# A three-layer mixer on one core: another order for the last batch of the first phase, and another buffer for w_ch

## The chip, the cores and the metric

The kernel runs on one core of a Trainium2 chip. The metric is the device time of one execution in microseconds. Three timed runs of the kernel before gave 1033.99, 1036.04 and 1035.72 us; the median is 1035.72 us.

## What is computed

The reference has eight batches of 576 tokens and 512 channels and three layers, each fed by the one ahead of it:

```python
q_s = softmax(q, axis=-1); k_s = softmax(k, axis=2)
x = q_s @ (k_s^T @ v)                       # by head; heads side by side: 576 x 512
u, v = split(relu(x @ w_in))                # 512 + 512 channels
v_n = (v - mean(v)) / sqrt(var(v) + 1e-6)
x = (u * (w_spatial @ v_n + b_spatial)) @ w_out
theta = x @ w_theta
y = w_tok_r @ (x * cos(theta)) + w_tok_i @ (x * sin(theta))
u = x + y
out = u + relu(u @ w_ch)
```

## The kernel before, in words

All products keep near fp32 accuracy: an operand is held as a high part in fp32r and a low part (`three`, L196), and a product is three matmuls. Weights are split on the chip once; those of the last layer wait in DRAM (`th_d`, `ch_d`, `op_d`).

The program has two phases. The first goes over the batches b = 0 to 7 (`run`, L1103) and does attention and the gated layer; its result, called y, goes to DRAM in four stores per batch (`y_out`, L656). The second goes over the batches again (`step2`, L1090) and does the last layer. The order of all work is written by hand, as words in strings: `PLANS`, `PLAN` and `LAST` (L33 to L75) for the first phase, `PLAN2` and `LAST2` (L57 to L68) for the second. Each word calls one function, and each engine works through its instructions strictly in the order in which the words issue them. A word that waits on an engine therefore holds up all later words on that engine; a DMA that POOL or SP issues stands in the queue of that engine too.

`LAST` is the plan of batch 7 of the first phase. There is no next attention to prepare, so it also carries the first steps of the second phase's batch 0, as words with an H ahead. Its words, in the order of the data:

- V, v, N: the five token tiles of x times the right half of w_in, relu, statistics and normalisation. U, r: the left half of w_in. S, G: the spatial product and the gate. Y, y: the product with w_out (`y_mm`, L647) and its store (`y_out`, L656: an ACT copy out of PSUM at L659, a DMA on SP at L660).
- ldy0, ldy1, ldr: loads of y of batches 0 and 1. th: the load of w_theta into the half of w_in's buffer that V has used (L1031). tok: the loads of the first token operators w11 and t2, of the rows that are left over and of their differences (L1032 to L1036, all DMAs of POOL).
- Hm0 to Hm4: theta of the five token tiles (`th_mm`, PE, L194). Hw, Ht, Hr: the turns, the reduction and the sine and cosine (L743 to L768, ACT and DVE). Hy: four transposes of y on PE (`th_y`, L774). Hz: the products x cos and x sin (`th_z`, DVE, L781, L782; tile 4 at L789). Hs, Hn, Hp, Hi, Hk, HI, HL: sums and the splits into high and low parts (L794 to L841, on ACT, DVE and POOL). Tile 4 holds the left-over tokens of two batches.

The scratch tiles of `t2` (L169) are nine buffers used in a ring: who takes one waits for the last user, a DMA that stores from it among them. In the first phase PSUM has three double banks (`big`, L163), used by S, Y and Hy among others, and two single banks for theta. Behind `LAST` the PSUM pools are made anew (L1130), and two operators that stay for the whole second phase are loaded over the gate's buffer (L1129).

The second phase does seven token products per batch (Q0 to Q6, `product`, L843, PE L867), then the product with w_ch in four parts (C0 to C3, `ch_mm`, L909; its weights are listed by `ch_pairs`, L902). The split parts zr and zi of x cos and x sin of tiles 2 and 3 lie in w_in's buffer for batch 0 and in w_out's for the later ones (`zs`, L666). w_ch is loaded once, in batch 0, by the word ldc (L1069) into the part of w_in's buffer in which those parts of batch 0 lie.

Of the kernel before, what the change touches and what calls it, by code (L numbers as in the profile page):

```python
# [17 lines left out]
P = 128  # L18
# [37 lines left out]
}  # L56
PLAN2 = (  # L57
# [5 lines left out]
)  # L63
# [4 lines left out]
)  # L68
LAST = (
# [5 lines left out]
)  # L75


OPS = ("w11", "t2", "w21", "t3", "t1", "t4", "w22")
# [3 lines left out]
def kernel(  # L82
# [15 lines left out]
    nc = tc.nc  # L98
    B = q.shape[0]
    S = w_tok.shape[2]  # L100
    D = 64
    DM = w_out.shape[2]
# [32 lines left out]
    w4_all = fix.tile([P, 8, 1024], F32R, name="w4")  # L135
    sp_all = fix.tile([P, 10, S], F32R, name="sp")
    g_all = fix.tile([P, 8, S], F32R, name="g")
    w4 = [w4_all[:, i, :] for i in range(8)]
    sp_w = [sp_all[:, i, :] for i in range(10)]
    g_s = [g_all[:, i, :] for i in range(8)]  # L140
    wo_all = fix.tile([P, 4, 1024], F32R, name="wo")
    wo = [wo_all[:, i, :] for i in range(4)]
# [13 lines left out]
    ch_d = dram.tile([P, 8, 512], F32R, name="ch_d")  # L156
# [21 lines left out]
    def f(ap):  # L178
        return ap.bitcast(F32)
# [16 lines left out]
    def three(a, w):  # L196
        return [(a[0], w[0]), (a[0], w[1]), (a[1], w[0])]
# [465 lines left out]
    y1 = [t.rearrange("p (k s) -> p k s", k=NK) for t in (qb, kb)]  # L663
    z_rem = [vn[8:10]]

    def zs(b, t):  # L666


        if t < 2:
            z = vn[4 * t:4 * t + 4]  # L670
        else:
            z = [w[:, 0:DM] for w in w4[4 * t - 8:4 * t - 4]]
            if b:
                z = [w[:, h * DM:(h + 1) * DM] for w in wo[2 * t - 4:2 * t - 2] for h in range(2)]
        return z[0:2], z[2:4]


# [10 lines left out]
    def op_load():  # L688
        n = turn["load"]
        if n < B * len(TURNS):  # L690
            nc.gpsimd.dma_start(out=op_buf[n % 2], in_=op_d[TURNS[n % len(TURNS)]])
            turn["load"] += 1
# [15 lines left out]
    th = {"phase": 0}  # L708
# [83 lines left out]
    LO, UP = slice(0, DM // 2), slice(DM // 2, DM)  # L792
# [20 lines left out]
    def th_hi(b, t):  # L813
        if t < NT:
            nc.scalar.copy(out=s2[t][0], in_=th["s2", b, t])
            nc.scalar.copy(out=zs(b, t)[0][0], in_=th[b, t][1])
        else:
            for full, z in zip(th[b, t], z_rem):
                nc.scalar.copy(out=z[0], in_=full)

    def th_zi_hi(b, t, eng):
        z, r = zs(b, t)[1][0], th[b, t][0]
        if eng is nc.gpsimd:
            eng.tensor_scalar(out=z, in0=r, scalar1=1.0, scalar2=0.0, op0=ALU.mult, op1=ALU.add)  # L824
        else:
            nc.scalar.copy(out=z, in_=r)

    def th_lo(b, t, eng):
        if t < NT:
            z, w = zs(b, t)[0], th[b, t][1]  # L830
            eng.tensor_tensor(out=z[1], in0=w, in1=f(z[0]), op=ALU.subtract)  # L831
        else:
            for full, z in zip(th[b, t], z_rem):
                nc.vector.tensor_tensor(out=z[1], in0=full, in1=f(z[0]), op=ALU.subtract)
# [58 lines left out]
    def s_late(b, n, t, hi, eng=None):  # L893
# [5 lines left out]
        else:  # L899
            eng.tensor_tensor(out=z[1], in0=x, in1=f(z[0]), op=ALU.subtract)  # L900

    def ch_pairs(m):  # L902
        pairs = []
        for kk in range(NK):
            w = w4[kk][:, m * P:(m + 1) * P], w4[4 + kk][:, m * P:(m + 1) * P]
            pairs += three(w, (st["uh"][:, kk, :], qt_s[kk]))
        return pairs

    def ch_mm(b, m):  # L909
        th["c", m] = big()  # L910
        acc(th["c", m], ch_pairs(m))
# [14 lines left out]
    def ch_half(b, m, h):  # L926

        c = (A, B_)[h]
        ps = bank()[:, A]
        acc1(ps, [(a, x[:, c]) for a, x in ch_pairs(m)])  # L930
        o = t2()[:, A]
        nc.vector.scalar_tensor_tensor(
            out=o, in0=ps, scalar=0.0, in1=y1[b % 2][:, m, c], op0=ALU.max, op1=ALU.add
        )
        nc.sync.dma_start(out=out[b, m][:, c], in_=o)
# [4 lines left out]
    w1 = {}  # L940
    for i in range(8):
        c = slice(i * P, (i + 1) * P)
# [5 lines left out]
    for i in range(NK):  # L948
        c, d = slice(i * P, (i + 1) * P), slice(DM + i * P, DM + (i + 1) * P)
# [39 lines left out]
    def hv(fl):  # L989
# [76 lines left out]
        "ldr": lambda b, i, fl: load_rem(b + 2),  # L1066
        "ldy": lambda b, i, fl: load_y(b + 2),
        "b": lambda b, i, fl: op_load(),
        "ldc": lambda b, i, fl: b or [  # L1069
            nc.gpsimd.dma_start(out=w4_all[:, :, c], in_=ch_d[:, :, c]) for c in (LO, UP)  # L1070
        ],
        "C": lambda b, i, fl: ch_mm(b, i),
        "o": lambda b, i, fl: ch_out(b, i, eng(fl, nc.vector)),
        "x": lambda b, i, fl: ch_half(b, i % 4, i // 4),
# [138 lines left out]
```

## Time and profile before

| what | us |
|---|---|
| median of three timed runs | 1035.72 |
| the profiled execution, its own time | 1033.3 |
| span of that profile | 1031.5 |
| busy: PE, DVE, ACT, POOL | 963.0, 783.7, 480.4, 505.0 |

The span is the time from the first instruction to the last. PE is busy for 93% of it. The page cuts the span into 40 slices of 25.8 us and gives each engine's busy tenths: PE's row has 9 nearly everywhere, 7 in the slices 22 and 23 (567 to 619 us) and 8 in slice 25. Batch 7 of the first phase runs from 520.8 to 606 us, batch 0 of the second from there to 665.2 us. A group's idle time before it and what ended it stand in brackets in the timeline.

### The profile page before, as it was taken

The numbers are of one execution on the slowest core, as the hardware profiler recorded it, in microseconds if no ns is written. First come the engines' busy times: TensorE is split into PE (matmuls) and PEld (weight loads), VectorE is DVE, ScalarE is ACT, GpSimd is POOL, SyncE is SP. The second block draws the span as 40 slices with busy tenths as digits, with TensorE's granted clock in tenths as the row PEclk, the third lists the DMA queues.
The fourth block names the chain that finished last, engine by engine and source line by source line (L and its number), as shares of the span: only waits on it lengthen the run. The fifth ranks groups of instructions, "written<-read, shape, count | busy, mean of one in ns | idle before, by whom it ended". The sixth has DMA issues, their size and how long they took to land.

```text
span 1031.5 us, 16589 instructions
## 1 busy us (share of the span) xinstructions
PE 963.0 (93%) x6496; PEld 908.4 (88%) x6496; DVE 783.7 (76%) x1156; ACT 480.4 (47%) x821; POOL 505.0 (49%) x502
## 2 busy tenths in 40 slices
PE   4587999999999999999999779899999999999998
PEld 3566899999899998999999669898999989998997
DVE  7888867778878788776435667879888878887874
ACT  3645546543555445554324443345454545354520
POOL 6366147555546565435112443637374645645460
PEclk9989999999999999999999989999999999999999
DMA  7541441425545175330150355642726253534432
GB/s 265 202 133 46 165 159 39 162 73 184 173 147 202 68 238 170 129 133 19 45 198 12 138 200 175 179 170 92 240 90 232 82 203 118 200 122 162 138 139 92
DMA packets 49998, 147.84 MB, mean 143 GB/s; under 512 B 8320, under 2 KB 23936, under 8 KB 40832
## 3 DMA queue, kind: packets, MB, share of 16 engines
q1 hardware_dynamic: 40464, 92.16, 25.7%
q0 software_dynamic: 9456, 54.63, 15.6%
q8 instruction: 51, 0.84, 0.3%
q14 instruction: 27, 0.22, 0.1%
HBM read 113.38 MB, written 33.39 MB: 142 GB/s over the span
## 4 chain that ended last, share of the span: by engine, by line
PE 58%; DVE 5%; POOL 4%; DMA 4%; issue 3%; ACT 1%; DVEq 0%; POOLq 0%; ACTq 0%
PE ps L186 25%; PE ps L867 15%; PE pb L194 9%; PE ps L194 5%; DMA sp<-op_t 2%; PE ps L446 1%; PE pb L774 1%; DMA y<-t 1%; DMA w<-ch_d 1%; PE ps L528 1%; DVE wo L831 1%; POOL s L811 1%; DMA sp<-op_w 1%; POOL s L810 0%; POOL wo L824 0%
## 5 line engine op out<-in xcount | busy, mean ns | idle before, releaser
L186 PE MATMUL ps<-sp,vn 128*128 128x288 f32 x896 | 127.9, 300 | 6.0 <-ACT vn L609 2.7
L186 PEld LDWEIGHTS ps<-sp,vn 128*128 128x128 f32 x896 | 121.7, 191 | 7.3 <-ACT vn L609 2.9
L186 PE MATMUL ps<-g,wo 128*128 128x288 f32 x768 | 109.2, 300 | 5.2 <-ACT t L659 4.6
L186 PEld LDWEIGHTS ps<-g,wo 128*128 128x128 f32 x768 | 104.6, 191 | 7.1 <-ACT t L659 5.7
L186 PE MATMUL ps<-xh,w 128*128 128x288 f32 x512 | 94.4, 302 | 9.1 <-ACT w L279 7.7
L194 PE MATMUL ps<-w,xh 128*128 128x512 f32 x320 | 97.5, 397 | 3.6 <-ACT t L581 2.8
L186 PEld LDWEIGHTS ps<-xh,w 128*128 128x128 f32 x512 | 78.0, 192 | 11.0 <-ACT w L279 7.9
L186 PE MATMUL ps<-uh,w 128*128 128x288 f32 x448 | 81.8, 299 | 3.7 <-DMA w<-ch_d 3.7
L194 PE MATMUL pb<-w,xh 128*128 128x512 f32 x256 | 80.3, 395 | 0.0
L194 PEld LDWEIGHTS ps<-w,xh 128*128 128x128 f32 x320 | 59.1, 188 | 17.5 <-ACT t L581 3.5
L186 PEld LDWEIGHTS ps<-uh,w 128*128 128x128 f32 x448 | 67.7, 191 | 4.9 <-DVE t L757 4.1
L645 POOL TENSOR_TENSOR g<-t,g 128x576 fp32r<-128x576 f32 x19 | 28.6, 1504 | 73.6 <-ACT g L644 73.5
L810 POOL TENSOR_TENSOR s<-t,t 128x256 f32<-128x256 f32 x32 | 25.1, 784 | 79.0 <-DVE t L805 79.0
L867 PE MATMUL ps<-sp,vn 128*128 128x288 f32 x360 | 59.3, 298 | 2.8 <-DMA sp<-op_w 1.2
L747 ACT ACTIVATE t<-pb 128x512 f32<-128x512 f32 x36 | 21.6, 599 | 73.6 <-PE pb L194 57.2
L186 PE MATMUL ps<-xl,w 128*128 128x288 f32 x256 | 55.7, 300 | 0.0
L194 PEld LDWEIGHTS pb<-w,xh 128*128 128x128 f32 x256 | 46.8, 188 | 9.6
L867 PEld LDWEIGHTS ps<-sp,vn 128*128 128x128 f32 x360 | 50.9, 188 | 4.2 <-issue 2.3
L644 ACT CAST g<-t 128x576 fp32r<-128x576 f32 x32 | 21.5, 673 | 69.6 <-DVE t L643 69.5
L867 PE MATMUL ps<-sp,s 128*128 128x288 f32 x384 | 53.7, 295 | 0.0
L867 PEld LDWEIGHTS ps<-sp,s 128*128 128x128 f32 x384 | 52.4, 188 | 0.6
L523 POOL TENSOR_TENSOR qb<-qb,q_s 128x512 f32<-128x512 f32 (+1 forms) x40 | 38.7, 1000 | 25.3 <-DVE q_s L517 21.6
(263 smaller groups left out, 2552.1 us busy)
## 6 DMA issues: line engine op xcount, KB each, us to landing
sp<-op_t POOLq DMA_DIRECT2D x24, 1152.0 KB, 5.7
sp<-op_w POOLq DMA_DIRECT2D x16, 1152.0 KB, 5.5
vb<-in_v SPq DMA_DIRECT2D x8, 1300.0 KB, 7.5
y<-t SPq DMA_DIRECT2D x32, 288.0 KB, 2.3
qb<-in_q SPq DMA_DIRECT2D x7, 1152.0 KB, 5.2
out<-t SPq DMA_DIRECT2D x28, 288.0 KB, 2.1
kb<-in_k SPq DMA_DIRECT2D x6, 1152.0 KB, 5.1
st<-in_w_tok SPq DMA_DIRECT2D x9, 576.0 KB, 4.0
```

The costliest lines, as they stand in the source:

```text
L186: nc.tensor.matmul(out=ps[:, c, 0:CH], lhsT=a, rhs=w[:, c * CH:(c + 1) * CH], start=first and i == 0, stop=final and i == last,)
L194: nc.tensor.matmul(out=ps, lhsT=a, rhs=w, start=(i == 0), stop=(i == last))
L446: nc.tensor.matmul(out=o, lhsT=kb[p, c0:c0 + P], rhs=v4[p, r, 2 * j:2 * j + 2, :].rearrange("p h e -> p (h e)"), start=(r == 0), stop=(r = ...
L523: eng.tensor_tensor(out=x, in0=x, in1=m.to_broadcast(list(x.shape)), op=ALU.mult)
L528: nc.tensor.transpose(ps[:, r * P:(r + 1) * P], qb[:, r * 512 + j * P:r * 512 + (j + 1) * P], ident)
L644: nc.scalar.copy(out=g_s[m], in_=g)
L645: eng.tensor_tensor(out=g_s[4 + m], in0=g, in1=f(g_s[m]), op=ALU.subtract)
L747: nc.scalar.activation(out=w, in_=ps, func=ACTF.Copy, scale=INV_2PI, bias=MAGIC)
L774: nc.tensor.transpose(yn[:, j * P:(j + 1) * P], y, ident)
L810: eng.tensor_tensor(out=th["s4"][:, t, :], in0=r[:, LO], in1=x, op=ALU.subtract)
L811: eng.tensor_tensor(out=th["s1"][:, t, :], in0=x, in1=w[:, LO], op=ALU.add)
L867: nc.tensor.matmul(out=ps[:, m, 0:CH], lhsT=a, rhs=x, start=i == 0, stop=i == len(pairs) - 1)
```

## The change

The plan `LAST` is another table. In it y's load of batch 0 stands first; the token products V, U and the theta steps of the tiles are interleaved in another way; the spatial products S2 and S3 stand ahead of the theta products Hm2 to Hm4, tok stands behind them on PE; and some steps go to other engines (a letter v sends a step to DVE, p to POOL, c to ACT). Second, w_ch is loaded into w_out's buffer by one DMA, and ldc stands earlier in batch 0 of `PLAN2`, behind the second operator load. Third, zr and zi of the tiles 2 and 3 lie in w_in's buffer for every batch.

```diff
 PLAN2 = (
...
-    "J3 b1 f3 e0 g2 G2v g1 g3 G1v i4c' d0 y0 J1 f2 y1 h0 Q3 g0 G0v J0 m0 w0 G3 F3v e1 a2v Q4 t0 r0 "
+    "J3 b1 ldc f3 e0 g2 G2v g1 g3 G1v i4c' d0 y0 J1 f2 y1 h0 Q3 g0 G0v J0 m0 w0 G3 F3v e1 a2v Q4 t0 "
...
 LAST = (
-    "V0 v0 V1 V2 v1 N0v B0p v2 V3 V4 v3 ldr th U0 r0 U1 v4 r1 N1 N2 U2 N3 N4v rsp B U3 r2 r3 ldy0 "
...
+        "ldy0 V2 v2 V0 v0 U1 N2v r1 V1 v1 N1v N0c V4 V3 v3 th U0 ldr v4 N4 B0 P0v B0s E0 E1v P E0 E1v "
...
     def zs(b, t):
...
             z = [w[:, 0:DM] for w in w4[4 * t - 8:4 * t - 4]]
-            if b:
-                z = [w[:, h * DM:(h + 1) * DM] for w in wo[2 * t - 4:2 * t - 2] for h in range(2)]
...
+    ch_w = wo_all.rearrange("p k (h c) -> p (k h) c", h=2)
+
     def ch_pairs(m):
...
-            w = w4[kk][:, m * P:(m + 1) * P], w4[4 + kk][:, m * P:(m + 1) * P]
+            w = ch_w[:, kk, m * P:(m + 1) * P], ch_w[:, 4 + kk, m * P:(m + 1) * P]
...
-        "ldc": lambda b, i, fl: b or [
-            nc.gpsimd.dma_start(out=w4_all[:, :, c], in_=ch_d[:, :, c]) for c in (LO, UP)
-        ],
+        "ldc": lambda b, i, fl: b or nc.gpsimd.dma_start(out=ch_w, in_=ch_d),
```

Between the plans the line numbers of the changed kernel shift by one or two. How the instructions stand on three engines follows; g is the gate's result, wo w_out's buffer, w_76 w_in's, sp the buffer of the spatial weights and then of the token operators, qb y of batch 0, yr the left-over tokens, vn, w_76 and s the split parts, t a scratch tile with its number.

PE at the end of `LAST`, before, from the last theta product to the first token product (L867):

```order
L194 MATMUL pb<-w_76,kvl 128x512
L186 MATMUL ps<-g,wo 128x288 x24
L774 MATMUL ps<-turned,qb 128x128 x4
L186 MATMUL ps<-g,wo 128x288 x24
L774 MATMUL ps<-turned,qb 128x128 x4
L186 MATMUL ps<-g,wo 128x288 x24
L774 MATMUL ps<-turned,yr 128x128 x4
L186 MATMUL ps<-g,wo 128x288 x24
L867 MATMUL ps<-sp,vn_80 128x288 x2
```

And now:

```order
L195 MATMUL pb<-w_76,kvl 128x512
L772 MATMUL ps<-turned,qb 128x128 x4
L187 MATMUL ps<-g,wo 128x288 x24
L772 MATMUL ps<-turned,qb 128x128 x4
L187 MATMUL ps<-g,wo 128x288 x72
L772 MATMUL ps<-turned,yr 128x128 x4
L865 MATMUL ps<-sp,vn_80 128x288 x2
```

The transposes of tile 4 (yr) stood ahead of the last of w_out's four products and stand behind it now; the other transposes stand ahead of the second product, with nothing between the last three.

POOL around the loads of tok, before, from the last gate on:

```order
L645 TENSOR_TENSOR g<-t_5652,g 128x576
L810 TENSOR_TENSOR s_5712<-t_5556,t_5713 128x256
L811 TENSOR_TENSOR s_5711<-t_5713,t_5557 128x256
L824 TENSOR_SCALAR vn_82<-t_5556 128x512
L838 TENSOR_TENSOR vn_83<-t_5556,vn_82 128x512
L691 DMA sp<-op_w_101 128x2304
L691 DMA sp<-op_t_102 128x2304
L1034 DMA sp<-rem_d 128x1152
L1035 DMA yr<-diff_d 128x576
L810 TENSOR_TENSOR s_5712<-t_5642,t_5773 128x256
```

And now:

```order
L646 TENSOR_TENSOR g<-t_5528,g 128x576
L689 DMA sp<-op_w_101 128x2304
L689 DMA sp<-op_t_102 128x2304
L1034 DMA sp<-rem_d 128x1152
L1035 DMA yr<-diff_d 128x576
L829 TENSOR_TENSOR vn_81<-t_5575,vn_80 128x512
L829 TENSOR_TENSOR vn_85<-t_5568,vn_84 128x512
L839 TENSOR_TENSOR s_5700<-t_5738,s_5700 128x256
L808 TENSOR_TENSOR s_5702<-t_5667,t_5849 128x256
```

The four loads stood behind the first tile's sums and splits on POOL and stand ahead of all of them now; the only thing that the first of them waits for is the last spatial product, whose weights it overwrites.

ACT behind the first copy of y out of PSUM, before, with tile 4's first step at L747:

```order
L816 CAST vn_80<-t_5557 128x512
L659 COPY t_5759<-ps 128x576
L747 ACTIVATE t_5768<-pb 128x512
L766 ACTIVATE t_5705<-t_5704 128x512
L767 ACTIVATE t_5704<-t_5704 128x512
L768 ACTIVATE t_5705<-t_5705,half_pi 128x512
L815 CAST s_5710<-t_5773 128x256
```

And now, with tile 4's first steps at L745 and L752:

```order
L660 COPY t_5766<-ps 128x576
L824 CAST vn_82<-t_5574 128x512
L813 CAST s_5700<-t_5738 128x256
L814 CAST vn_84<-t_5568 128x512
L824 CAST vn_86<-t_5567 128x512
L764 ACTIVATE t_5736<-t_5735 128x512
L765 ACTIVATE t_5735<-t_5735 128x512
L766 ACTIVATE t_5736<-t_5736,half_pi 128x512
L745 ACTIVATE t_5843<-pb 128x512
L660 COPY t_5845<-ps 128x576
L752 ACTIVATE t_5843<-t_5843 128x512
```

Seven steps now come between the first copy of y (t_5766) and tile 4's first step (t_5843), which takes that copy's scratch buffer; the second copy of y (t_5845) stands behind it.

## Rows read from the trace of the kernel before

**Rows 1.** The page's first line.

```profile
span 1031.5 us, 16589 instructions
```

**Rows 2.** Chain of waits: start us, us, engine, output and line, instructions; DMA: what landed.

```profile
520.78 13.07 PE ps L194 x56
533.86 20.25 PE ps L186 x152
554.11 5.61 PE pb L194 x24
559.72 7.45 PE ps L186 x56
...
576.45 3.21 PE ps L186 x24
580.40 9.92 DMA y<-t
...
639.60 8.66 DMA w<-ch_d
```

**Rows 3.** Timeline, end of the first phase: start, us, instruction [idle before <- what ended it].

```profile
577.35 1.29 POOL L838 TENSOR_TENSOR vn<-t,vn 128x512 fp32r<-128x512 f32 x1
577.62 1.57 DVE L758 SCALAR_TENSOR_TENSOR t<-t,t 128x512 f32<-128x512 f32 x1
578.59 0.65 POOL L691 DMA_DIRECT2D sp<-op_w  x1
...
590.45 0.69 DVE L757 SCALAR_TENSOR_TENSOR t<-t,pb 128x512 f32<-128x512 f32 x1 [7.18 <-DMA y<-t]
591.17 0.69 DVE L758 SCALAR_TENSOR_TENSOR t<-t,t 128x512 f32<-128x512 f32 x1
...
595.42 1.09 PE L774 MATMUL ps<-turned,yr 128*128 128x128 f32 x4 [8.54 <-issue]
...
600.33 4.84 PE L186 MATMUL ps<-g,wo 128*128 128x288 f32 x24 [3.82 <-ACT t L659]
...
605.95 0.40 PE L867 MATMUL ps<-sp,vn 128*128 128x288 f32 x1 [0.78 <-ACT t L659]
```

**Rows 4.** Timeline, PE at the first product with w_ch.

```profile
648.39 0.82 PE L186 MATMUL ps<-uh,w 128*128 128x288 f32 x2 [3.67 <-DMA w<-ch_d]
...
649.49 1.16 PE L186 MATMUL ps<-uh,w 128*128 128x288 f32 x4
...
653.46 0.69 PE L186 MATMUL ps<-uh,w 128*128 128x288 f32 x4
```

**Rows 5.** Busy time by stretch: PE, PEld, DVE, ACT, POOL, granted clock, DMA share, GB/s.

```profile
590.00:600.00 10.00, 1.09 (x4) 0.72 (x4) 9.33 (x15) 3.88 (x8) 4.90 (x6) 0.50 0.00 1
...
520.80:606.00 85.20, 72.06 (x441) 65.83 (x440) 49.28 (x83) 35.29 (x61) 29.35 (x33) 0.92 0.32 108
606.00:665.20 59.20, 54.75 (x364) 51.73 (x364) 41.41 (x56) 23.57 (x45) 27.70 (x31) 0.97 0.63 200
721.00:773.10 52.10, 51.93 (x353) 49.12 (x353) 44.54 (x65) 24.73 (x47) 26.27 (x28) 1.00 0.48 165
```

**Rows 6.** DMA issues from 500 to 700 us: count, size, median us to landing.

```profile
y<-t SPq DMA_DIRECT2D x8, 288.0 KB, 2.2
...
w<-th_d POOLq DMA_DIRECT2D x1, 2048.0 KB, 9.2
```

**Rows 7.** Groups by line from 575 to 608 us: count | busy, mean ns.

```profile
L789 DVE TENSOR_TENSOR t<-t,ps 64x512 f32<-64x512 f32 x4 | 2.7, 684 | 0.1
L659 ACT COPY t<-ps 128x576 f32<-128x576 f32 x4 | 2.5, 638 | 5.9 <-PE ps L186 5.9
...
L767 ACT ACTIVATE t<-t 128x512 f32<-128x512 f32 x3 | 1.9, 632 | 0.1
...
L815 ACT CAST s<-t 128x256 fp32r<-128x256 f32 x4 | 1.6, 394 | 3.7 <-DVE t L805 3.7
...
L805 DVE TENSOR_TENSOR t<-t,t 128x256 f32<-128x256 f32 x3 | 1.3, 425 | 0.2
```

More of the change, by code (lines that the diff above doesn't have):

```diff
@@ L69 @@
 LAST = (
[5 rows of a table removed]
-)
[6 rows of a table added]
+    )
 OPS = ("w11", "t2", "w21", "t3", "t1", "t4", "w22")
```

11 rows, old and new, of tables (LAST, PLAN2) are left out of this document.

## The prediction

> **What bounds the kernel now.** I read the page first: a span of 1031.5 us [rows 1] in an execution of 1033.3 us, so 1.8 us lie around the span and I leave them as they are. The chain of waits shows what ends last: from 520.78 us, where batch 7 of the first phase begins on PE, it is PE work without a gap for 55 us [rows 2]. Then it stops being PE: a store of y takes 9.92 us in the chain, and later the load of w_ch takes 8.66 us [rows 2]. The busy time by stretch shows how much is at stake: 72.06 busy us in the 85.20 us of the last first-phase batch, 54.75 in the 59.20 us of the first second-phase batch, but 51.93 in 52.10 us for a later batch of the same work [rows 5]. So only these two stretches have something to give.
>
> The timeline names the holes. POOL issues the token loads at 578.59; the store of y's first part, 288 KB, starts behind them at 580.40 and lands 9.92 us later, where the median of such stores is 2.2 us [rows 2, 3, 6]. DVE's L757 for tile 4 has to take that store's scratch buffer and waits 7.18 us, until 590.45 [rows 3]. All that DVE has behind it (tile 3's products, which free a PSUM bank) waits too, and PE stands for 8.54 us before tile 4's transposes, 3.82 us before the last w_out product and 0.78 us before the first token product [rows 3]. Behind the waits the clock is low: granted 0.50 in 590 to 600 us, the level of 1.2 GHz [rows 5]; the 24 matmuls that take 3.21 us at 2.4 GHz [rows 2] take 4.84 [rows 3], 1.6 us more. In the next batch PE waits 3.67 us for w_ch, and then four matmuls take 1.16 us where four later ones take 0.69 [rows 4]; I take another 1.6 us for that.
>
> **PE's own work in the last batch.** The work is the same before and after. From the chain [rows 2]: V 13.07, U with S0 and S1 20.25, two theta products 5.61, S2 and S3 7.45; three more theta products at half of 5.61 each, 8.41; four w_out products at 3.21, 12.84; five sets of transposes at about a third of 1.09 us each (that row ran at half clock and its end overlaps), 1.75. Sum 69.4 us. The batch took 605.95 - 520.78 = 85.2 us, so 15.8 us were lost: 13.1 us of the three waits, about 2 us of slow clock, the rest small.
>
> **The new order, stage by stage.** Times stand on the clock of the trace of before.
>
> V, U and S. V2 goes first instead of V0, which needs no more than V0 did. The splits of vn are what S0 waits for, and they are spread over ACT, DVE and POOL now. The last of them, vn7 on POOL, comes about 0.2 us before S0 asks for it when I add up ACT's queue; a 512-wide step of POOL is 1.29 us [rows 3], so this costs 0 to 1.3 us, and I take 0. The load of w_theta is issued behind V3, about 541 us, and lands 9.2 us later [rows 6], 550; the first theta product comes at 554.1. Y's load stands first on SP, some 20 us ahead of its first reader: nothing.
>
> Theta, S2, S3. PE order is two theta products, S2 and S3, three theta products. The gate's DVE and ACT steps for S0 and S1 fall into 551 to 556 us and so free PSUM before S2 and S3 ask. Nothing is added. The token loads are now issued when S3 ends, about 567.5, instead of 578.59. In the trace everything of them and the store were through 11.7 us after the first issue (590.3 - 578.59), so now they are through at about 579.3.
>
> w_out's products. Through the first one PE is at 520.78 + 13.07 + 20.25 + 5.61 + 7.45 + 8.41 + 3 x 0.35 + 3.21 = 579.8. The second needs the first one's bank, which the ACT copy (0.64 [rows 7]) gives back: PE waits to 580.6, with one set of transposes inside the wait. Three products of 3.21 follow, to 590.2. Their banks come from tile 2's products (DVE, about 583.5, asked for at 583.8) and the second copy (586, asked for at 587).
>
> The store of the first part leaves at 580.6, behind loads that are through, and lands 2.2 us later, 582.8. Tile 4's first ACT step takes its buffer, but seven steps stand ahead of it: six of 0.63 and one of 0.39 [rows 7], to 584.7. So the wait that cost 7.18 us has 1.9 us to spare.
>
> The new tail. From 584.7 ACT does tile 4's first step, the second copy and L752, 1.9 us, to 586.6. DVE then does L755 to L757 (0.69 + 0.69 + 0.43 [rows 3, 7]) to 588.4, one short split 0.42, tile 3's two products 1.36, to 590.2: this frees the bank for tile 4's transposes, just when PE has finished w_out. Then come L802, L803 (0.85), L829 (0.68) and the four products of tile 4 at 0.68 [rows 7], to 594.5. The first token product waits for these, since the new PSUM pools need the old banks, so PE stands from 590.6 on. **This is the stall that takes the place of the old ones.** The second pair of these products takes the buffer of the third copy; that store leaves at 591.1 and lands at 593.3, which adds 0.2 us.
>
> What the rows say of DVE beside POOL: L758 took 1.57 us while POOL's L838 ran for 1.29, against 0.69 alone [rows 3]. In 582 to 591 us POOL now has steps of this kind. Bounds: 0, and all of POOL's work there, three 512-wide steps of 1.29 and three half as long, 5.8 us. Ahead of L755 DVE is through at about 585.2 and waits for ACT until 586.6, which takes up 1.4 us of such holds, so I take 1.5 us, nearer to the low end. The token product starts at 594.7 + 1.5 = 596.2, against 605.95: 9.75 us gained. PE has then stood for over 5 us and I charge one slow start, 1.6 us (bounds 0 and 2).
>
> **The first batch of the second phase.** w_ch's load is issued behind the second operator load, some 35 us before its first reader; 8.66 us [rows 2] are far inside. The wait of 3.67 us and its slow start of 1.6 go: 5.3 us. The check from the other side: the batch from its twelfth matmul (605.95 + 1.6) to 665.2 is 57.6 us, a later batch 52.1 [rows 5], a difference of 5.5. One DMA for two saves POOL under 1 us, off the path. On the 16 DMA engines the load now runs beside the operator loads that Q3 and Q4 need: 0 to 8.66 us. The operator of Q4 is issued before it and needed about 11 us later, so I take 0.
>
> From batch 1 on, zr and zi lie in the other buffer with the same readers and the same order of waits: nothing.
>
> **Sum:** 9.75 - 1.6 + 5.3 = 13.45 us, so 1033.3 - 13.45 = 1019.9 us. The timed runs lie 0.7 to 2.7 us above the profiled execution; by their median it would be 1022.3. I say 1021, and put the other cases on the same level, 1.1 above their sums.
>
> **Rivals.**
>
> *The port between DVE and POOL (1025).* If every POOL step of the tail holds DVE for its full length, 5.8 us instead of 1.5, the token product starts 4.3 us later: 1024.2, on the level 1025. For it: L758 ended just behind L838 [rows 3]. Against: the gap of 1.4 us there. The Trainium skill, page "SBUF — State Buffer", section "Who interferes with whom", says that a DVE step with two SBUF inputs and a GpSimd step that reads SBUF exclude each other for a whole instruction; by that rule this case would hold wherever the two meet. The trace agrees at the one place shown.
>
> *A store still behind loads (1028).* If the first or the third store takes 9.92 us again, tile 4 ends 7.7 us later: 1027.6, on the level 1028. It needs loads that last to 581 us, or the gate's buffer to be reloaded before 593; POOL comes to that reload only behind tile 3's sums, about 593.5, so the margin is the length of one store.
>
> *w_ch moves its wait (1026).* If its load holds up Q3 or Q4 for as long as C0 waited, the 5.3 us come back: 1025.2, on the level 1026.
>
> *The order is worth nothing (1035).* A wait in V, U or S that I took for covered eats the gain: w_theta or the splits of vn late by over 10 us. Every row speaks against it, since the margins are small but the waits are short.
>
> *Slower: the clock (1044).* After the stall of 5 us the clock is at 1.2 GHz. In the trace of before it is back within the next 24 matmuls (1.6 us lost of 3.2 possible [rows 3]). If it stayed low in the first token batch, each us of its 52 us of PE work [rows 5] would cost one more. From 13.5 us of such work on nothing is gained, half a batch gives 1019.9 - 1.6 + 26 = 1044. Before, granted clock is 0.97 in that batch [rows 5], so there is no sign of it. The Trainium skill, page "TensorE: Matmul & The Clock Gate", section "HAM oscillation — how this bites in real kernels", describes a kernel in which short bursts between waits kept falling back to the low clock. No such row stands here.
>
> **Numbers.** Forecast 0.55; port 0.18; store 0.13; w_ch 0.06; nothing gained 0.04; slower 0.04. A difference of 0.2% (2 us) is about what a measurement can tell. Faster: 0.55 + 0.18 + 0.13 + 0.06 = 0.92; same 0.04; slower 0.04. The range goes from 1016 (no hold of DVE by POOL and no slow start, 3.1 us less than the sum, near 1017.8, less a little of unknown spread) to 1029 (the store).
>
> **What would show it.** Right: no DVE wait on a store of y of more than 1 us; w_out's last three products without a gap over 0.5 us; one PE wait of 4 to 7 us before the first token product, ended by DVE's products of tile 4; no PE wait on w_ch; that batch near 53.5 us. Wrong: a PE wait in V to S3, a store of y over 5 us, a wait on an operator load in Q3 or Q4, or a granted clock under 0.9 in the whole first token batch.

## The result, and the profile after

The changed kernel takes 1019.31 us in the median of four runs (1018.24 to 1020.64), the kernel before 1035.88 us beside it. The ratio is 0.9843 with an interval of 0.9824 to 0.9861: 14 to 18 us faster. The forecast was 1021, with a range of 1016 to 1029. The four runs of the kernel before lie rather high here: beside the later runs its median was 1033.7 to 1034.53 us, and by a repeat of the changed kernel (e5 below) the gain is 12 to 17 us.

The profiled execution took 1020.64 us. The page of the changed kernel, its first line and PE's total, which was 963.0 us before: PE does the same work and stands less.

```profile
span 1018.9 us, 16589 instructions
...
PE 962.1 (94%) x6496; PEld 907.6 (89%) x6496; DVE 779.2 (76%) x1158; ACT 484.8 (48%) x828; POOL 495.5 (49%) x496
```

The chain of waits of the changed kernel (start us, us, engine, output and line, instructions), the counterpart of [rows 2]:

```profile
523.42 5.60 PE ps L195 x24
...
556.73 2.81 PE pb L195 x12
...
594.68 0.68 DVE t L787
596.09 0.69 DVE t L787
596.79 0.70 DVE t L787
597.73 11.95 PE ps L865 x78
...
650.60 0.76 DVE t L920
651.35 0.90 DVE w L829
```

No DMA stands in this stretch of it any more. Batch 7 of the first phase starts at 523.42 and the first token product at 597.73: 74.31 us, against 605.95 - 520.78 = 85.17 before. The chain leaves PE behind the second theta product and runs through DVE and ACT up to tile 4's products (L787).

The waits of PE from 520 to 665 us in the changed kernel (engine, line, what it waited for: us, times, longest):

```profile
PE ps L865 <- DVE t L787: 4.0, 1, 4.0
PE ps L187 <- ACT t L660: 0.3, 1, 0.3
```

Before, there were five: 8.5, 3.8, 0.8, 3.7 [rows 3, 4] and 0.7 us for a token operator. Now one of 4.0 us is left. The timeline of the changed kernel around it, several engines together (start, us, instruction [idle before <- what ended it]):

```profile
570.00 0.62 POOL L689 DMA_DIRECT2D sp<-op_w  x1 [13.95 <-PE ps L187]
...
583.42 11.07 SPq L661 DMA_DIRECT2D y<-t  x4
583.45 9.84 PE L187 MATMUL ps<-g,wo 128*128 128x288 f32 x72 [0.29 <-ACT t L660]
...
588.71 0.69 DVE L755 SCALAR_TENSOR_TENSOR t<-t,pb 128x512 f32<-128x512 f32 x1
...
593.13 0.60 PE L772 MATMUL ps<-turned,yr 128*128 128x128 f32 x4
594.68 2.80 DVE L787 TENSOR_TENSOR t<-t,ps 64x512 f32<-64x512 f32 x4
597.73 1.78 PE L865 MATMUL ps<-sp,vn 128*128 128x288 f32 x6 [4.01 <-DVE t L787]
599.31 1.53 PE L865 MATMUL ps<-sp,w 128*128 128x288 f32 x6
...
602.29 3.36 PE L865 MATMUL ps<-sp,s 128*128 128x288 f32 x24
```

The token loads are issued at 570.00, y's first store at 583.42. DVE takes up tile 4 at 588.71 with no wait in brackets, where [rows 3] had 7.18 us. The last three products with w_out run through (72 matmuls in 9.84 us). PE then stands from 593.7 until L787 is done, and the first token matmuls are slow: 4.56 us from 597.73 to 602.29 for 24 of them, with a granted clock of 0.52 from 597.7 to 600.7 us, the level of 1.2 GHz in nearly all of that stretch. The DMA issues of the changed kernel from 568 to 585 us (count, KB each, us to landing):

```profile
sp<-op_w POOLq DMA_DIRECT2D x1, 1152.0 KB, 5.5
sp<-op_t POOLq DMA_DIRECT2D x1, 1152.0 KB, 7.7
sp<-rem_d POOLq DMA_DIRECT2D x1, 576.0 KB, 8.6
yr<-diff_d POOLq DMA_DIRECT2D x1, 288.0 KB, 8.8
y<-t SPq DMA_DIRECT2D x1, 288.0 KB, 2.1
```

The last load is issued at 571.66 and lands at 580.5; the store leaves 3 us later and takes 2.1 us, not 9.92. The busy time by stretch of the changed kernel (PE, PEld, DVE, ACT, POOL, granted clock, DMA share, GB/s), the counterpart of [rows 5]:

```profile
523.40:597.70 74.30, 70.03 (x441) 64.09 (x439) 43.83 (x80) 39.18 (x68) 22.57 (x29) 1.00 0.39 131
597.70:651.40 53.70, 53.67 (x359) 51.34 (x360) 42.60 (x61) 23.91 (x46) 24.36 (x27) 0.97 0.57 207
```

**A yardstick.** Single runs of one kernel spread by 1 to 7 us, so in each profile I also read two stretches that do not contain the start of the program: A, from the first matmul of batch 7 to the first token product, and B, from there to the DVE split (L829 here, L831 before) for which the next batch's first product waits. Before: A = 85.17, B = 664.36 - 605.95 = 58.41, together 143.58 us. After: 74.31 + 53.62 = 127.93. So 15.65 us come from these two stretches: 10.86 from the first, 4.79 from the second. The two profiled times differ by only 1033.3 - 1020.64 = 12.7 us, because this execution came to batch 7 2.64 us later, through code that the change doesn't touch (see the last section), and took 0.35 us more behind B.

### The profile page after: what moved, and what is told of

The parts are those of the page before. It is cut to its first block, busy times and chain, and to the rows that moved or that the text cites. A ratio compares the mean times of both kernels' runs of the same rounds, so it can differ in the third digit from the quotient of the medians.

```text
span 1018.9 us, 16589 instructions
## 1 busy us (share of the span) xinstructions
PE 962.1 (94%) x6496; PEld 907.6 (89%) x6496; DVE 779.2 (76%) x1158; ACT 484.8 (48%) x828; POOL 495.5 (49%) x496
## 4 chain that ended last, share of the span: by engine, by line
PE 55%; DVE 9%; POOL 5%; DMA 2%; issue 2%; ACT 1%; DVEq 0%; POOLq 0%; ACTq 0%
PE ps L187 21%; PE ps L865 17%; PE pb L195 8%; PE ps L195 5%; PE ps L447 1%; DVE t L802 1%; PE pb L772 1%; DMA sp<-op_t 1%; POOL s L808 1%; POOL w L822 1%; PE ps L529 1%; DMA qb<-in_q 1%; DVE t L779 1%; POOL s L809 1%; DVE t L756 1%
## 5 line engine op out<-in xcount | busy, mean ns | idle before, releaser
L187 PE MATMUL ps<-uh,wo 128*128 128x288 f32 x448 | 80.8, 296 | 0.0
L187 PEld LDWEIGHTS ps<-uh,wo 128*128 128x128 f32 x448 | 66.8, 188 | 0.9
L745 ACT ACTIVATE t<-pb 128x512 f32<-128x512 f32 x36 | 21.5, 598 | 70.7 <-PE pb L195 54.4
L808 POOL TENSOR_TENSOR s<-t,t 128x256 f32<-128x256 f32 x30 | 23.8, 792 | 64.2 <-DVE t L803 64.2
L646 POOL TENSOR_TENSOR g<-t,g 128x576 fp32r<-128x576 f32 x17 | 25.4, 1495 | 56.5 <-ACT g L645 56.4
L865 PE MATMUL ps<-sp,w 128*128 128x288 f32 x288 | 48.8, 301 | 3.9 <-DVE w L829 3.4
```

What stands on the lines that cost most here:

```text
L187: nc.tensor.matmul(out=ps[:, c, 0:CH], lhsT=a, rhs=w[:, c * CH:(c + 1) * CH], start=first and i == 0, stop=final and i == last,)
L646: eng.tensor_tensor(out=g_s[4 + m], in0=g, in1=f(g_s[m]), op=ALU.subtract)
L745: nc.scalar.activation(out=w, in_=ps, func=ACTF.Copy, scale=INV_2PI, bias=MAGIC)
L808: eng.tensor_tensor(out=th["s4"][:, t, :], in0=r[:, LO], in1=x, op=ALU.subtract)
L865: nc.tensor.matmul(out=ps[:, m, 0:CH], lhsT=a, rhs=x, start=i == 0, stop=i == len(pairs) - 1)
```

## The experiments

| run | kernel | A | B | A + B | median us |
|---|---|---|---|---|---|
| | before | 85.17 | 58.41 | 143.58 | 1035.88 |
| | changed | 74.31 | 53.62 | 127.93 | 1019.31 |
| e1 | new `LAST` alone | 74.32 | 62.47 | 136.79 | 1024.07 |
| e2 | w_ch's move alone | 84.47 | 53.02 | 137.49 | 1027.7 |
| e3 | changed, token loads late | 81.02 | 53.91 | 134.93 | 1025.58 |
| e4 | before, own buffer for y | 79.05 | 60.28 | 139.33 | 1029.53 |
| e5 | changed, again | 74.33 | 53.94 | 128.27 | 1019.25 |
| e6 | changed, own buffer for y | 74.07 | 53.84 | 127.91 | 1018.47 |
| e7 | changed, PE kept busy | 74.34 | 52.34 | 126.68 | 1018.29 |
| e8 | bank for tile 4, early loads | 70.77 | 54.39 | 125.16 | 1015.75 |
| e9 | e8 with a quiet POOL | 70.77 | 53.82 | 124.59 | 1014.85 |
| e10 | e8, again | 70.77 | 54.41 | 125.18 | 1014.47 |

The kernel before ran beside each set of runs: 1033.8 us beside e1 to e4, 1033.7 beside e5 to e8, 1034.53 beside e9 and e10.

**e1, the new order alone** (the kernel before with the new `LAST`; w_ch, zr and zi as they were):

```diff
 LAST = (
-    "V0 v0 V1 V2 v1 N0v B0p v2 V3 V4 v3 ldr th U0 r0 U1 v4 r1 N1 N2 U2 N3 N4v rsp B U3 r2 r3 ldy0 "
...
+        "ldy0 V2 v2 V0 v0 U1 N2v r1 V1 v1 N1v N0c V4 V3 v3 th U0 ldr v4 N4 B0 P0v B0s E0 E1v P E0 E1v "
...
```

> The kernel before with the new plan LAST alone; w_ch stays in w_in's buffer and is loaded where it was. Theory (two separate gains, one in each stretch): the last first-phase batch lasts 74 to 75 us instead of 85, the wait of some 3.7 us on w_ch and its slow start stay in the first token batch; time near 1025, 10 to 11 us under the kernel before. Rival (one gain: the load of w_ch decides both): the token batch pulls ahead only when w_ch moves, time within 3 us of the kernel before or within 2 us of the changed kernel.

Ratio 0.9918, interval 0.9893 to 0.9943. A is that of the changed kernel to 0.01 us: this half of the gain is the order's alone. But B grew by 4.1 us against the kernel before. The waits of PE in this kernel from 520 to 665 us, and its busy time by stretch:

```profile
PE ps L187 <- DMA w<-ch_d: 5.4, 1, 5.4
PE ps L868 <- DVE t L790: 4.0, 1, 4.0
```

```profile
596.64:659.11 62.47, 57.07 (x360) 54.51 (x361) 43.77 (x61) 23.95 (x46) 26.20 (x28) 0.90 0.57 177
```

The wait for w_ch is 5.4 us now, not 3.67, and the granted clock of the batch is 0.90: the 48 matmuls behind that wait take 8.52 us instead of 7.88, and the first 24 token matmuls, behind the stall of 4.0 us, take 5.85 us against 3.28 before. A batch that starts earlier doesn't bring w_ch earlier by as much: counted from batch 7's first matmul, the first token product starts 10.85 us earlier and the first product with w_ch 7.42.

**e2, w_ch's move alone** (the changed kernel with the old `LAST`, the reverse of the diff of e1).

> The changed kernel with the old plan LAST: only w_ch's buffer, its load's place and the place of zr and zi are new. Theory: the last first-phase batch keeps its 85 us and its stand of 7 us on a store of y, no wait on w_ch, the first token batch 5 to 6 us shorter; time 5 to 6 us under the kernel before, near 1030. Rival: the wait on w_ch is covered by another wait behind it (DVE's splits of the next batch), time within 2 us of the kernel before.

Ratio 0.9944, interval 0.9925 to 0.9964. B fell by 5.39 us; the sum had 5.3. The waits of PE from 520 to 665 us keep the old ones in A (the first is 7.3 us instead of 8.5; the store took 8.65 us here, not 9.92) and lose the one for w_ch:

```profile
PE ps L771 <- issue: 7.3, 1, 7.3
PE ps L186 <- ACT t L659: 3.8, 1, 3.8
PE ps L864 <- ACT t L659: 0.8, 1, 0.8
PE ps L864 <- DMA sp<-op_t: 0.4, 1, 0.4
```

So both halves count, and in the profiles they do not simply add: 6.79 us from the order and 6.09 from w_ch are 12.88 of the 15.65. With the new order w_ch's move is worth 136.79 - 127.93 = 8.86 us. The chains of the two profiles say where these are: 5.4 us of wait for w_ch, 8.52 - 6.36 = 2.16 in the 48 matmuls behind it, and 13.23 - 11.95 = 1.28 in the first 78 token matmuls, which stand behind the same stall of 4.0 us in both. So the part that doesn't add up is a longer wait for w_ch and slower matmuls behind both waits. By the medians alone the halves add up (9.7 and 6.1); e1's runs lie between 1023.17 and 1029.97, and this doesn't settle 3 us.

**e3, the token loads late** (the changed kernel with tok behind the first tile's split on POOL):

```diff
-... Hp0 Hm4 Hy3 tok HL0 Hz1 "
-"Hw3 Hs1 Y0 y0 Ht3 Hy2 Hz2 Hi0c Y2 Y3 Hk0p HI0v Hn1v ...
+... Hp0 Hm4 Hy3 HL0 Hz1 "
+"Hw3 Hs1 Y0 y0 Ht3 Hy2 Hz2 Hi0c Y2 Y3 Hk0p tok HI0v Hn1v ...
```

> The changed kernel with the word tok behind the first tile's split, so that POOL issues the four token loads about 581 to 583 us, just ahead of the first store of y, instead of at 570. Theory (the loads in front of y's stores are what stood in the way): the first store takes 8 to 10 us instead of 2, ACT's first step of tile 4 and the second copy wait for it, PE stands 5 to 8 us more before the first token product; time 5 to 9 us over the changed kernel, 1025 to 1028. Rival (the order on DVE and ACT made the gain, the place of the loads makes none): the store is late but nothing waits, time within 2 us of the changed kernel.

Ratio 0.9918, interval 0.9887 to 0.995: about 6 us over the changed kernel, and A + B 7.0 over it. The timeline of this kernel:

```profile
577.21 0.62 POOL L689 DMA_DIRECT2D sp<-op_w  x1
...
589.18 0.60 ACT L745 ACTIVATE t<-pb 128x512 f32<-128x512 f32 x1 [5.74 <-DMA y<-t]
...
590.36 4.98 PE L187 MATMUL ps<-g,wo 128*128 128x288 f32 x24 [3.96 <-ACT t L660]
...
592.49 0.69 DVE L755 SCALAR_TENSOR_TENSOR t<-t,pb 128x512 f32<-128x512 f32 x1 [7.41 <-DMA y<-t]
```

And its DMA issues from 568 to 585 us:

```profile
yr<-diff_d POOLq DMA_DIRECT2D x1, 288.0 KB, 11.0
y<-t SPq DMA_DIRECT2D x1, 288.0 KB, 9.4
```

Counted from batch 7's first matmul, the loads are issued 10.9 us later (57.48 against 46.58) and the same store takes 9.4 us. While it is under way, from 579.7 to 589.2 us, the 16 DMA engines are busy for 94% of the time, as in the kernel before (94% from 580.4 to 590.4); in the changed kernel, from 583.4 to 585.5, it is 37%. ACT's first step of tile 4 (L745) waits 5.74 us for the store's buffer, the second copy of y and a product with w_out wait behind it, and DVE, which takes up tile 4 behind ACT, stands for 7.41 us where [rows 3] had 7.18. With the rest of the new order untouched, this one delay brings the old wait back. A still stays 4.15 us under that of the kernel before: so much the rest of the new order is worth with the loads late, and it was not taken apart.

**e4, the kernel before with a buffer of its own for y** (the copies of batch 7 go to v's buffer, which is free there, so that the ring waits for no store; the loads stay late):

```diff
-        y = t2()
+        y = t2() if b < B - 1 else vb[:, m * S:(m + 1) * S]
```

> The kernel before with one edit: in the last first-phase batch y's four copies out of PSUM go to v's buffer, which is free by then, so that no scratch buffer waits for a store of y. Order and loads as before. Theory (the stand of DVE on the store's buffer is the root): the 7.18 us wait of DVE L757 is gone, the waits of PE of 8.5 and 3.8 us shrink to 2 to 6 us together, time 6 to 9 us under the kernel before, 1027 to 1030. Rival (PSUM banks or the token loads themselves bound PE there): PE waits as long, time within 2 us of the kernel before.

Ratio 0.996, interval 0.9943 to 0.9977: 4.3 us, less than the 6 to 9 expected. A fell by 6.1 us, but B rose by 1.9. The waits of PE from 520 to 665 us:

```profile
PE ps L186 <- ACT vb L659: 4.3, 1, 4.3
PE ps L186 <- DMA w<-ch_d: 4.1, 1, 4.1
PE ps L774 <- issue: 2.3, 1, 2.3
PE ps L867 <- ACT vb L659: 0.7, 1, 0.7
PE ps L867 <- DMA sp<-op_t: 0.5, 1, 0.5
```

The store still takes 9.1 us, and nobody waits for it: the wait was the ring's. Under it lies a second limit of the old order, DVE and ACT themselves, at 7.3 us of PE's standing (4.3 + 2.3 + 0.7). In the new order, which gives other steps to each of them, 4.0 us are left. In B the wait for w_ch is 0.4 us longer and the 48 matmuls behind it take 9.36 us in the chain, where they took 7.88 before and take 6.36 without a wait.

**e5 to e8** ran on one chip. **e5** is the changed kernel itself.

> The changed kernel as it is, as the yardstick for the three kernels beside it: a ratio to the kernel before of 0.982 to 0.987, so 1016 to 1022 us. Every theory says the same.

1019.25 us, ratio 0.9861, interval 0.9836 to 0.9885.

**e6, the changed kernel with y's copies in v's buffer** (the edit of e4).

> The changed kernel with y's four copies of the last batch in v's buffer, so that no scratch buffer of the ring waits for a store. Theory (in the changed order the token loads are through when y's first store leaves, and the ring's wait for it has slack): same as the changed kernel, within 1 us. Rival (the ring still costs something in the changed kernel, as tile 4's steps take the buffers of the first and third copies): 1 to 2 us faster, and the wait of 4.0 us before the first token product shrinks by as much.

1018.47 us, ratio 0.9848, interval 0.9824 to 0.9871, the same as e5; A + B is 0.36 us less than in e5 and that of the changed kernel's first profile, and PE's wait is 3.8 us instead of 4.0. The ring costs next to nothing in the changed kernel. What was worth 4 us in the old order is worth nothing in the new one.

**e7, PE kept busy in the wait** (12 theta matmuls more, whose result nobody reads, behind tile 4's transposes):

```diff
-... Hk2 HI2 Hy4 Hz4 Hn3 ...
+... Hk2 HI2 Hy4 warm Hz4 Hn3 ...
```

> The changed kernel with 12 more theta matmuls (about 2.8 us at full clock, products that nobody uses) on PE behind tile 4's transposes, inside the 4.0 us wait ahead of the first token product. Theory (the first 12 token matmuls are slow because PE stood still before them): the token product starts at the same time, its first 12 matmuls take about 1.9 us instead of 3.3, and the time falls by 1.0 to 1.4 us. Rival A (the slow start belongs to the first token product itself, by its operands or the new PSUM pools): first matmuls as slow as before, same time. Rival B (the added matmuls end late, or hold up DVE by the bank they take): slower by 0.5 to 2 us.

1018.29 us, ratio 0.9848, interval 0.9823 to 0.9873: by the runs alone it can't be told from e5. The timeline of this kernel, PE, shows the effect:

```profile
598.84 1.04 PE L868 MATMUL ps<-sp,vn 128*128 128x288 f32 x6 [1.22 <-DVE t L790]
599.71 0.98 PE L868 MATMUL ps<-sp,w 128*128 128x288 f32 x6
600.53 0.96 PE L868 MATMUL ps<-sp,vn 128*128 128x288 f32 x6
601.32 0.95 PE L868 MATMUL ps<-sp,w 128*128 128x288 f32 x6
602.11 3.36 PE L868 MATMUL ps<-sp,s 128*128 128x288 f32 x24
```

The same first 24 matmuls take 602.11 - 598.84 = 3.27 us, against 4.56 in the changed kernel's profile. A is unchanged to 0.03 us, B 1.28 us less than in that profile. The granted clock is 1.00 from 598.8 to 602.1 us. So the slow start belongs to PE's standing still, neither to the operands nor to the new PSUM pools. Its price is 1.3 us in that profile, and it isn't fixed: behind a stall of 3.8 to 4.2 us the same 24 matmuls take 4.78 us in e3 and e5, 4.79 in e6 and 5.85 in e1. In e5 the first six still run at the high clock (1.00 from 595.3 to 596.3 us) and the next ones don't (0.54 from 596.3 to 600.0).

**e8, the last stall** (three edits beside that of e6: tile 4's transposes into a single PSUM bank, its products behind tile 3's splits, the loads of the two operators that stay right behind tile 2's splits):

```diff
-        yn = bank() if th["phase"] else big()[:, 0, :]
+        yn = bank() if th["phase"] or t == NT else big()[:, 0, :]
...
-... Hk2 HI2 Hy4 Hz4 Hn3 Hp3 HL3 Hs4 Hn4 Hi4 HI4v Hp4 HL4p Hi3 Hk3 "
-"HI3v HI1v Hk4 "
+... Hk2 HI2 kept Hy4 Hp3 Hk3 HL3 Hz4 Hn3 Hs4 Hn4 Hi4 HI4v Hi3 HI3v HI1v Hp4 HL4p Hk4 "
```

> The changed kernel with three edits at its one remaining stall: tile 4's four transposes go to a single PSUM bank that is free, tile 4's products are placed behind tile 3's splits, and the loads of the two operators that stay are issued behind tile 2's split; y's copies of the last batch go to v's buffer. Theory (PE stands for 4.0 us because the new PSUM pools wait for DVE's products of tile 4, which are queued behind tile 3's): the first token product waits only for tile 3's products and y's last copies, the stall falls from 4.0 to about 1 us or less and the slow start goes with it, so 3 to 5 us under the changed kernel, 1014 to 1016.5 us, ratio about 0.980. Rival (the token products then wait for their own operands, tile 4's splits or the operators loaded earlier beside the stores): the wait moves into the first or second token product, same time as the changed kernel within 1 us.

1015.75 us, ratio 0.9821, interval 0.9799 to 0.9843, 3.5 us under e5. A is 3.6 us less: the first token product starts 0.46 us after PE is through with the transposes. But it then stands once, inside. The timeline of this kernel, DVE, POOL and PE:

```profile
593.83 0.77 POOL L803 TENSOR_TENSOR s<-t,t 128x256 f32<-128x256 f32 x1
594.08 2.33 DVE L824 TENSOR_TENSOR w<-t,w 128x512 fp32r<-128x512 f32 x1 [0.53 <-ACT w L809]
594.53 0.75 POOL L804 TENSOR_TENSOR s<-t,t 128x256 f32<-128x256 f32 x1
595.23 0.64 POOL L817 TENSOR_SCALAR w<-t 128x512 fp32r<-128x512 f32 x1
...
596.47 0.40 PE L860 MATMUL ps<-sp,w 128*128 128x288 f32 x1 [1.48 <-DVE w L824]
```

DVE's split of tile 3 stands beside three steps of POOL and ends 0.5 us after the last of them. What each of e8's three edits does by itself was not tried.

**e9, e8 with those three steps taken off POOL** (the sums to DVE behind tile 4's products, the cast to ACT):

```diff
-... Hz4 Hn3 Hs4 Hn4 Hi4 HI4v Hi3 HI3v ...
+... Hz4 Hn3v Hi3c Hs4 Hn4 Hi4 HI4v HI3v ...
```

> The kernel of e8 with three steps of POOL taken out of the tail: tile 3's two sums go to DVE, behind tile 4's products, and the cast of its zi to ACT. In e8 DVE's split of tile 3's zr took 2.33 us while these three steps ran on POOL, against 0.69 us for the same split alone, and PE waited 1.48 us for it. Theory (a DVE step that reads two operands from SBUF stands still for the whole of POOL's steps beside it): that split takes 0.7 us, the wait in the first token product goes, and the time falls by about 1.5 us under e8, near 1014 us. Rival (the split was long for another reason, such as the two operator loads that POOL had just issued): it takes over 2 us again and the time is that of e8 within 0.5 us.

The timeline of this kernel:

```profile
590.25 0.69 DVE L824 TENSOR_TENSOR w<-t,w 128x512 fp32r<-128x512 f32 x1 [0.52 <-ACT w L809]
...
602.10 1.06 PE L860 MATMUL ps<-sp,vn 128*128 128x288 f32 x6 [0.82 <-DMA sp<-op_t]
```

The split takes 0.69 us and PE's wait for it is gone: shown. The rival, the two loads that POOL has just issued, is out, since POOL issues them ahead of the split here too. The gain is not: 1014.85 us against 1014.47 of **e10**, e8 again beside it (ratios 0.9805, interval 0.9781 to 0.983, and 0.9799, interval 0.9776 to 0.9821).

> The kernel of e8 unchanged, as the yardstick for e9 on the same chip: ratio to the kernel before of 0.980 to 0.984, so 1014 to 1017.5 us. Every theory says the same.

In A + B e9 is 0.6 us better, not 1.5: now the third token product waits 0.82 us for its operator, whose 8.68 us of transfer stand in the chain. So the split went as the theory said and the time as the rival said.

e8, run twice, beats both kernels: 18 to 20 us under the kernel before, 3.5 us under the changed one on the same chip (3.1 us in A + B). e9 can't be told from it.

## Why the prediction was right, step by step

I put the changed trace on the clock of the one before by taking off 2.64 us.

- **The token loads earlier, the store's wait gone.** Forecast: loads issued at about 567.5, through at 579.3, the store leaves at 580.6. Measured: 567.36, 577.8, 580.8. e3 turns this one step back and gets a store of 9.4 us, a DVE wait of 7.41 us and 7.0 us of A + B: this cause is shown. The rival "store still behind loads" was priced at 7.7 us; e3 is that rival. The prediction put PE's three waits down to the store alone; e4 takes the store's wait away from the old order, and 7.3 of the 13.1 us stay, behind DVE's own work. The forecast didn't suffer by this, since it rebuilt DVE's queue step by step.
- **PE up to the end of w_out.** Forecast 590.2 for the end of the four products; measured 593.13 - 2.64 = 590.5. The gap in front of the second was 0.29 us, not 0.4. V, U and S cost nothing in their new order: from the batch's first matmul to the first theta product it is 556.73 - 523.42 = 33.31 us, and 33.33 before [rows 2]. The waits in A fell from 13.1 to 4.3 us [rows 3], the matmuls slowed behind the old waits [rows 3] were 2.1 us (4.84 against 3.21, 1.09 against 0.60), and 8.8 + 2.1 comes within 0.1 of the 10.86 us that A lost. What the new order of V, U and S does by itself was not tried.
- **The new tail and its stall.** Named rightly: PE stands before the first token product, released by tile 4's products. Forecast 5.6 us, measured 4.0. The DVE chain without any holds came out at 594.7; the product started at 595.09. The holds (the time by which a DVE step beside POOL's steps is longer than alone) were larger than the 1.5 us taken: L836 1.36 us, one L808 0.96, one L757 0.85 and one L839 0.82, against 0.68, 0.42, 0.43 and 0.42 alone, 2.0 us in all. But 1.2 us of it lie ahead of L755, where they cost next to nothing, since DVE and ACT came to L755 within 0.1 us of each other; it began at 586.07, not at 586.6. So **the mis-sized term** is "so I take 1.5 us": 0.8 us of holds came behind L755, and 0.4 us more than the chain without holds reached PE.
- **The slow start.** Forecast 1.6 us, measured 1.3 (e7), and six matmuls take 0.96 us, full speed, from 600.7 us on, 3 us after the product began. Behind nearly the same stall it was 1.5 us in e3, e5 and e6 and 2.6 in e1, so that 1.3 came out near 1.6 is in part luck. The rival in which the clock stays low through half a batch is excluded: the granted clock of B is 0.97. (Its break-even was misread: with the 1.6 us taken off as in its own sum, nothing is gained from 15 us of slow work on, not from 13.5.)
- **w_ch.** Forecast 5.3 us; e2 measured 5.39. No wait on w_ch, on the operators of Q3 or Q4, so the rival "w_ch moves its wait" is excluded. B fell by 4.8 where 5.3 - 1.6 = 3.7 was due: the slow start is 0.3 us less, and a wait of 0.7 us for a token operator that the kernel before had, and that I had not counted, is gone.
- **The port.** As a rival priced at the whole of POOL's work it is excluded, since PE stood 4.0 us. As a mechanism it is confirmed by e8 and e9: 2.33 us beside POOL, 0.69 without. The Trainium skill, page "SBUF — State Buffer", section "Who interferes with whom", says that a DVE step with two SBUF inputs and a GpSimd step that reads SBUF exclude each other for one whole instruction. The trace agrees that they hold each other up (2.33 us against 0.69), but the hold in e8 lasted through three POOL steps in a row (0.77, 0.75 and 0.64 us), so the length of one instruction was not its bound here.

The sum was 13.45 us; A + B gained 15.65, of which 1.1 us more than forecast in A and 1.1 in B. The sum made against the profiled execution (1019.9) and the median of the runs (1019.31) agree to 0.6 us partly by luck: the gain was larger than the sum, and the profile of before lay 2.6 us under the median of its four runs, though only 0.4 to 1.2 us under the medians of its later runs.

## What to carry to other kernels

Where a scratch ring feeds a store, look at which loads are under way when the store leaves: 288 KB took 2.1 us with no load under way and 9.4 us behind 3.1 MB of loads, and the engine that took the buffer next passed nearly all of it on. Either the loads go earlier (e3 against the changed kernel: 7 us) or the store gets a buffer outside the ring (e4: 6 us in that stage). And read a wait's successor before pricing its removal: under the store's wait lay a DVE limit that kept PE standing for 7 us, and under the new order's stall one of POOL against DVE, then one of an operator's load, each of a size that the profile shows only when the one above is gone.

## What the runs showed that I had not expected

Most of the spread between profiles lies at the start of the program, in code that all the kernels share. In the twelve profiles SP issues the first store of y between 115.18 us (e9) and 120.93 us (e7), with the same code ahead of it. From there to the first of the four stores ahead of batch 7's own it takes 393.0 to 393.1 us in eleven of them and 393.4 in e5. From the end of B to the end of the execution they differ by 1.3 us. A difference of 2 us between two kernels in one profile each means nothing until this is taken off; stretches A and B repeat to 0.4 us (changed and e5) and to 0.02 (e8 and e10).

The price of a wait on PE is not the wait alone, and it varies: behind a wait for w_ch of 3.67 us the next 48 matmuls took 7.88 us, behind 4.10 us 9.36 (e4), behind 5.40 us 8.52 (e1), and 6.36 us without a wait. What decides it was not tried.
